# Retention and a mish feed-forward layer in one kernel: chunk steps of the first tiles reordered, states evacuated by ScalarE, four more chunks transposed by TensorE, the last tile's outputs in swapped banks

## The chip, the cores and the metric

The kernel runs on one core of one Trainium2 chip. The metric is device time in microseconds (us) of one execution. A profiled execution has a span, from its first to its last instruction; its own time is a little longer than the span.

## The reference

Two layers follow each other. The first is a retention layer: attention without softmax, with a causal mask and a decay for each head. Its output, as 4608 tokens of 512 features, goes through a feed-forward layer with the activation mish, h * tanh(softplus(h)).

```python
# q, k, v: (8 batches, 8 heads, 576 positions, 64), float32
scores = scale * q @ k.T                                # scale = 1/sqrt(64)
gamma = 1.0 - 2.0 ** (-5.0 - arange(8))
Dmat = where(i >= j, gamma ** (i - j), 0.0)
x = ((scores * Dmat) @ v).transpose(0, 2, 1, 3).reshape(4608, 512)
h = x @ w_in                                            # 512 -> 2048
out = (h * tanh(softplus(h))) @ w_out                   # 2048 -> 512
```

## The kernel before

**Chunks and tiles.** The tokens are cut into 36 chunks of up to 128 positions. A chunk holds all eight heads. Each batch has four chunks of 128 (c = 0 to 3); the remaining 64 positions of two neighbouring batches share a fifth (c = 4). Four chunks make a tile of 512 tokens, so there are nine tiles, 0 to 8; chunk n belongs to tile n // 4.

**The decay.** gamma ** (i - j) is split into a factor for q, gamma ** i (`gq`), and one for v, gamma ** -j (`gv`). What is left for the scores is the plain causal mask, and what earlier chunks give to a later one is a running state k.T v for each head, 64 x 64, summed in one PSUM bank, `st`.

**The steps of a chunk n.** They are small functions, and `att(n, "PSKO")` calls those that its letters name:

- P (`prep`): GpSimd (POOL) casts k into `qks`, VectorE (DVE) scales q into `qks`, GpSimd scales v into `vs`. For n over 8, P also issues the loads of up to two later chunks, as far as chunk n + 7 (`more_loads`).
- T (`step_t`): q and k are transposed, two heads at a time, into `qkT`. For n below `NPE` = 12 TensorE does it in eight matmuls with the identity, into a PSUM bank (from the pool `hp` for tile 0, from `sc` later), and ScalarE (ACT) copies the result (L183). For other chunks a DMA transpose, issued by ScalarE, does it (L185).
- S (`step_s`): eight matmuls give the scores in two PSUM banks (`sc`, one of two such pairs), and VectorE multiplies them by the mask into `sm` (L200).
- K (`step_k`): eight matmuls add this chunk to the state in `st`. VectorE reads `st` and writes `ssb` (L221): of each pair of heads, one copy where the lower half of the partitions is zeroed, one where the upper half is, by a multiplication with `diag`. The next K may not write `st` before that read is done. Chunks with c = 4 have no K.
- O (`step_o`): for c > 0 eight matmuls (sixteen for c = 4) multiply the earlier state by the transposed q, and eight multiply `sm` by `vs`, all into the first `sc` bank. VectorE copies the result into `xT`, the tile's input of the feed-forward layer (L246).

**The feed-forward layer.** `g1(t, f)` multiplies tile t by 128 columns of w_in, four matmuls of 512 columns into a bank `hp` (one of two), and ScalarE takes the mish of it into `gT` (L259). `g2(t, i)` is a quarter of one chunk's product with w_out, four matmuls into the bank `ops`, and after the last quarter VectorE copies the result to `res` (one of three) and SyncE (SP) issues the store (L280). In the last tile, 8, every second chunk's output goes to an `hp` bank instead of `ops`.

**Order.** Everything is in the order in which the code is written: each engine runs its instructions in that order, and each of SP's DMA issues waits for its turn and for its inputs. There are five parts:

1. Attention of tile 0, chunk by chunk.
2. All of `g1(0, ...)`, with the casts of w_in, by GpSimd, between them.
3. The f loop (L328): the products of the first three chunks of tile 0 with w_out, in the order in which w_out's eight pieces arrive and are cast (L115), one piece for two steps; three banks collect the sums. The steps of chunks 4 to 7 stand between them, four values of f for a chunk.
4. Tile 1: the last quarter of tile 0's product (`g2(0, 12)` to `g2(0, 15)`), and `g1(1, ...)` with the steps of chunks 8 to 11.
5. Tiles 2 to 8, and a last round without `g1`: `g1(t, i)` and `g2(t - 1, i)` alternate, and the steps of two chunks of tile t + 1 stand in each half of 16 rounds.

Of the kernel before, what the change touches and what calls it, by code (L numbers as in the profile page):

```python
# [12 lines left out]
AX = mybir.ActivationFunctionType  # L13
OP = mybir.AluOpType
# [3 lines left out]
def kernel(  # L18
# [25 lines left out]
    nF = d_ff // P  # L44
    KC = d_model // P
    NCH = 4
    NPE = 12


    chunks = []  # L50
# [5 lines left out]
    nT = len(chunks) // NCH  # L56
# [8 lines left out]
    op = ctx.enter_context(tc.tile_pool(name="op", bufs=3))  # L65
# [85 lines left out]
    diag = consts.tile([P, 2], F32)  # L151
# [7 lines left out]
    live = {}  # L159
    xts = {}  # L160

    def prep(n):
        b, c = chunks[n]
        qr, kr, vr = raw.pop(n)
        qks = tok.tile([P, 2, H, D], BF16, name="qks")
        vs = tok.tile([P, H, D], BF16, name="vs")
        nc.gpsimd.tensor_copy(qks[:, 1], kr)  # L167
        nc.vector.tensor_tensor(qks[:, 0], qr, gq[:, c, :].unsqueeze(2).to_broadcast([P, H, D]), op=OP.mult)  # L168
        nc.gpsimd.tensor_tensor(vs, vr, gv[:, c, :].unsqueeze(2).to_broadcast([P, H, D]), op=OP.mult)  # L169
        live[n] = (qks, vs)  # L170

    def step_t(n):
        qks, vs = live[n]
        flat = qks.rearrange("p i h d -> p (i h d)")
        qk = tr.tile([P, 2, NP, P], BF16, name="qkT", bufs=5)
        if n < NPE:
            if n < NCH:
                tp = ps_h.tile([P, 2 * NP, P], BF16, name="hp")
            else:
                tp = ps_sc.tile([P, 4 * NP, P], BF16, name="sc")[:, 0:2 * NP]  # L180
            for i in range(2 * NP):
                nc.tensor.transpose(tp[:, i, :], flat[:, ts(i, P)], ident)  # L182
            nc.scalar.copy(qk.rearrange("p i n t -> p (i n) t"), tp)  # L183
        else:
            nc.scalar.dma_start_transpose(out=qk.rearrange("p i n t -> p (i n) t"), in_=flat)  # L185
        live[n] = (qk, qks[:, 1], vs)

    def step_s(n):

        b, c = chunks[n]  # L190
        qk, ks, vs = live[n]
        sc = ps_sc.tile([P, 2, NP, P], F32, name="sc")
        for p in range(NP):
            for e in range(2):
                r = ds(64 * e, 64)
                nc.tensor.matmul(sc[:, e, p, :], lhsT=qk[r, 1, p, :], rhs=qk[r, 0, p, :],  # L196
                                 start=True, stop=True)
# [5 lines left out]
        live[n] = (qk, ks, vs, sc, sm)  # L203

    def step_k(n):

        if n >= len(chunks):
            return
        b, c = chunks[n]
        if c == 4:  # L210
            return
        ks, vs = live[n][1:3]
        if c == 0:
            st_ps[b] = ps_st.tile([P, NP, 64], F32, name="st")
        st = st_ps[b]
        for p in range(NP):
            for e in range(2):
                nc.tensor.matmul(st[ds(64 * e, 64), p, :], lhsT=ks[:, 2 * p + e, :], rhs=vs[:, 2 * p + e, :],  # L218
                                 start=(c == 0 and p == 0), stop=True, skip_group_check=True)
        ssb = tr.tile([P, NP, 2, 64], BF16, name="ssb", bufs=8)  # L220
        nc.vector.tensor_tensor(  # L221
            ssb, st.unsqueeze(2).to_broadcast([P, NP, 2, 64]),
            diag.unsqueeze(1).unsqueeze(3).to_broadcast([P, NP, 2, 64]), op=OP.mult)
        st_sb[b, c] = ssb

    def step_o(n):

        b, c = chunks[n]
        t, s = divmod(n, NCH)
        qk, ks, vs, sc, sm = live.pop(n)  # L230
# [13 lines left out]
        if s == 0:  # L244
            xts[t] = xp.tile([P, KC, NCH * P], BF16, name="xT")
        nc.vector.tensor_copy(xts[t][:, :, ts(s, P)], ot)  # L246
# [14 lines left out]
    def g2(t, i):  # L261
        s, part = divmod(i, 4)
        if part == 0:
            if t == nT - 1 and s % 2:
                outs[t] = ps_h.tile([P, d_model], F32, name="hp")
            else:
                outs[t] = ps_o.tile([P, d_model], F32, name="ops")
        ops = outs[t]
        for f in range(4 * part, 4 * part + 4):
            nc.tensor.matmul(ops, lhsT=gts[t][:, f, ts(s, P)], rhs=w_out_t[:, f, :],  # L270
                             start=(f == 0), stop=(f == nF - 1))
        if part == 3:
            store(t, s, ops, nc.vector.tensor_copy)
# [51 lines left out]

    accs = [ps_h.tile([P, NCH * P], F32, name="hp") for _ in range(2)]
    accs += [ps_o.tile([P, d_model], F32, name="ops")]
    for f in range(nF):  # L328
        n, w = NCH + f // 4, f % 4
        if w == 0:  # L330
            att(n, "PT")
        elif w == 1:
            att(n, "SK")
        elif w == 3:
            att(n, "O")
        if f % 2 == 0:
            j = f // 2
            cast_w("out", j)
            if j + STG < 8:
                load_w("out", j + STG)  # L340
            if j == 1 or j > 3 and j != 5:
                more_loads(10, 1)
        for s in range(3):
            nc.tensor.matmul(accs[s], lhsT=gts[0][:, f, ts(s, P)], rhs=w_out_t[:, f, :],
                             start=(f == 0), stop=(f == nF - 1))
    att(2 * NCH, "PT")
    for s in range(3):
        store(0, s, accs[s], nc.vector.tensor_copy if s % 2 else nc.scalar.copy)

    for i in range(nF):  # L350
        n, w = 2 * NCH + i // 4, i % 4
        if i < 4:
            g2(0, 12 + i)
        if w == 0:
            att(n + 1, "P")
            att(n, "SK")
        elif w == 2:
            att(n, "O")
            att(n + 1, "T")
        if n + 2 == NPE + 1:  # L360
            if w == 1:
                att(n + 2, "P")
            elif w == 3:
                att(n + 2, "T")
        g1(1, i)

    for t in range(2, nT + 1):
        for i in range(nF):
            n, w = NCH * (t + 1) + i // 8 * 2, i % 8
            if t < nT:  # L370
                if w == 0:
                    att(n, "S")
                    att(n + 1, "S")
                    if n == NPE:
                        att(n, "K")
                elif w == 1 and n == NPE:
                    att(n + 1, "K")
                if w in (0, 2):
                    att(n + 2 + w // 2, "P")
                elif w in (1, 3):  # L380
                    att(n + 2 + w // 2, "T")
                elif w == 4:
                    att(n + 2, "K")
                    att(n, "O")
                    att(n + 1, "O")
                    att(n + 3, "K")
                g1(t, i)
            g2(t - 1, i)

# [29 lines left out]
```

## Time and the profile before

| | us |
|---|---|
| median of 3 runs | 347.21 (346.68 to 348.35) |
| profiled execution, own time | 347.57 |
| its span | 345.9 |
| TensorE busy (matmuls) | 307.6, 89% of the span |
| VectorE busy | 131.1, 38% |
| ScalarE busy | 100.7, 29% |
| GpSimd busy | 79.0, 23% |
| mean granted clock of TensorE | 0.988 |

Rows of the profile name an instruction by its line in the code, its engine, the tile that it writes and those that it reads. PE is TensorE (PEld its weight loads, which overlap the matmuls), DVE VectorE, ACT ScalarE, POOL GpSimd; SPq and ACTq are DMA issues by SP and ScalarE. A row of the timeline gives the start, the length, the instruction and how many of its kind were merged (x8), and, in brackets, how long the engine had stood idle before it and what ended the wait. A row by stage gives start and end, length, busy time of PE, PEld, DVE, ACT and POOL with their instruction counts, the granted clock, and the mean busy share and rate of the DMA engines. A row of the chain has start, length and instruction only.

### The profile page before, as it was taken

Reading aid. Unit: us, or ns where it says so; the run is one execution under the profiler, and the core shown is the slowest. Engines: PE = TensorE matmul, PEld = TensorE weight load, DVE = VectorE, ACT = ScalarE, POOL = GpSimd, SP = SyncE. Lnnn points to the kernel's source line nnn. Section 1 sums busy time; section 2 is a strip of 40 time slices with the busy share of each in tenths; the row PEclk is TensorE's granted clock in tenths of the full one; section 3 lists DMA queues with packets and bytes.
Section 4 is the critical chain, followed back from the end, with each engine's and each line's share of the span. In section 5 each row is a group of like instructions: output and inputs, shape, how many; then the busy total and the mean of one; then the engine's idle time right before and its main releaser. Section 6 shows DMA issues by size and latency. Waiting matters only on the chain.

```text
span 345.9 us, 5710 instructions
## 1 busy us (share of the span) xinstructions
PE 307.6 (89%) x2336; PEld 148.4 (43%) x2336; DVE 131.1 (38%) x186; ACT 100.7 (29%) x163; POOL 79.0 (23%) x100
## 2 busy tenths in 40 slices
PE   2458988689979996999999999999999999999994
PEld 1343434344534442444444445444554444444441
DVE  2662035615653421635344342434353633001111
ACT  4122641226512232132222323223222232333200
POOL 4566554514411311213030303030301000000000
PEclk9999999989989999999999999999999999999999
DMA  9999999999897989999794949473140411000122
GB/s 172 226 349 260 303 250 246 174 215 204 142 201 127 209 168 254 247 184 204 174 221 108 229 110 203 98 119 89 36 91 32 99 54 31 32 30 30 48 75 61
DMA packets 149530, 52.80 MB, mean 153 GB/s; under 512 B 138752, under 2 KB 142848, under 8 KB 149504
## 3 DMA queue, kind: packets, MB, share of 16 engines
q1 hardware_dynamic: 124160, 46.15, 60.9%
q10 hardware_dynamic: 25344, 6.29, 11.3%
q8 instruction: 18, 0.29, 0.4%
q14 instruction: 8, 0.07, 0.1%
HBM read 36.70 MB, written 9.44 MB: 133 GB/s over the span
## 4 chain that ended last, share of the span: by engine, by line
PE 65%; DMA 13%; SPq 8%; DVE 6%; issue 3%; POOL 2%; ACT 2%; ACTq 1%; DVEq 0%; POOLq 0%
PE hp L257 29%; PE ops L270 27%; SPq L85 7%; DMA wst<-in_moe_w_out_dram 5%; DVE res L277 2%; DMA wst<-in_moe_w_in_dram 2%; PE sc L196 2%; PE hp L270 2%; DMA qkT<-qks 2%; DVE ssb L221 2%; DMA vraw<-in_v_dram 1%; DMA qraw<-in_q_dram 1%; PE st L218 1%; DVE qks L168 1%; DMA out_dram<-res 1%
## 5 line engine op out<-in xcount | busy, mean ns | idle before, releaser
L257 PE MATMUL hp<-xT,w_in_t 128*128 128x512 bf16 x576 | 149.1, 389 | 1.3 <-DVE xT L246 0.8
L259 ACT ACTIVATE gT<-hp 128x512 bf16<-128x512 f32 x144 | 84.9, 597 | 187.3 <-PE hp L257 166.9
L270 PE MATMUL ops<-w_out_t,gT 128*128 128x512 bf16 x496 | 127.2, 381 | 6.3 <-DVE res L277 4.2
L257 PEld LDWEIGHTS <-w_in_t 128*128 128x128 bf16 x576 | 54.6, 99 | 67.0 <-issue 7.2
L270 PEld LDWEIGHTS <-gT 128*128 128x128 bf16 x528 | 52.0, 98 | 70.4 <-issue 10.0
L277 DVE COPY res<-ops 128x512 f32<-128x512 f32 x31 | 21.5, 692 | 149.4 <-PE ops L270 139.6
L169 POOL TENSOR_TENSOR vs<-vraw,gv 128x512 bf16<-128x512 f32 x36 | 38.0, 1057 | 127.6 <-issue 66.2
L200 DVE TENSOR_TENSOR sm<-sc,mask 128x1024 bf16<-128x1024 f32 x36 | 43.0, 1219 | 34.8 <-PE sc L196 34.7
L167 POOL CAST qks<-kraw 128x512 bf16<-128x512 f32 x36 | 23.2, 644 | 42.3 <-DMA kraw<-in_k_dram 31.2
L246 DVE CAST xT<-sc 128x512 bf16<-128x512 f32 x36 | 23.7, 685 | 13.7 <-PE sc L242 13.7
L168 DVE TENSOR_TENSOR qks<-qraw,gq 128x512 bf16<-128x512 f32 x36 | 24.8, 711 | 4.6 <-DMA qraw<-in_q_dram 4.6
L221 DVE TENSOR_TENSOR ssb<-st,diag 128x512 bf16<-128x512 f32 x32 | 21.8, 682 | 0.9 <-PE st L218 0.9
L196 PE MATMUL sc<-qkT 64*128 64x128 bf16 x288 | 13.6, 232 | 6.2 <-ACT qkT L183 3.5
L196 PEld LDWEIGHTS <-qkT 64*128 64x128 bf16 x288 | 8.8, 100 | 16.2 <-ACT qkT L183 6.7
L182 PE MATMUL hp<-ident,qks 128*128 128x128 bf16 x32 | 4.3, 310 | 12.6 <-DVE qks L168 11.9
L242 PE MATMUL sc<-sm,vs 128*64 128x128 bf16 x288 | 14.6, 230 | 0.0
L182 PEld LDWEIGHTS <-qks 128*128 128x128 bf16 x96 | 6.7, 111 | 18.4 <-DVE qks L168 16.9
L183 ACT COPY qkT<-sc 128x1024 bf16<-128x1024 bf16 x8 | 8.1, 1011 | 21.4 <-PE sc L182 21.4
L218 PE MATMUL st<-vs,qks 128*64 128x64 bf16 x256 | 10.6, 207 | 3.7 <-DVE ssb L221 3.7
L237 PE MATMUL sc<-qkT,ssb 128*64 128x128 bf16 (+1 forms) x256 | 12.0, 224 | 1.0 <-DVE sm L200 1.0
L218 PEld LDWEIGHTS <-qks 128*64 128x64 bf16 x256 | 7.2, 116 | 11.1 <-issue 10.4
L242 PEld LDWEIGHTS <-vs 128*64 128x64 bf16 x288 | 10.6, 117 | 1.0 <-issue 1.0
(34 smaller groups left out, 71.1 us busy)
## 6 DMA issues: line engine op xcount, KB each, us to landing
qraw<-in_q_dram SPq DMA_DIRECT2D x32, 256.0 KB, 5.0
kraw<-in_k_dram SPq DMA_DIRECT2D x32, 256.0 KB, 5.1
vraw<-in_v_dram SPq DMA_DIRECT2D x32, 256.0 KB, 5.1
out_dram<-res SPq DMA_DIRECT2D x32, 256.0 KB, 2.2
wst<-in_moe_w_in_dram SPq DMA_DIRECT2D x8, 512.0 KB, 6.1
wst<-in_moe_w_out_dram SPq DMA_DIRECT2D x8, 512.0 KB, 5.3
qraw<-in_q_dram SPq DMA_DIRECT2D x8, 128.0 KB, 4.2
kraw<-in_k_dram SPq DMA_DIRECT2D x8, 128.0 KB, 4.0
```

Source lines behind the costliest of these rows:

```text
L85: nc.sync.dma_start(out=t, in_=src[b, :, ds(P * c, P), :].rearrange("h p d -> p h d"))
L168: nc.vector.tensor_tensor(qks[:, 0], qr, gq[:, c, :].unsqueeze(2).to_broadcast([P, H, D]), op=OP.mult)
L169: nc.gpsimd.tensor_tensor(vs, vr, gv[:, c, :].unsqueeze(2).to_broadcast([P, H, D]), op=OP.mult)
L196: nc.tensor.matmul(sc[:, e, p, :], lhsT=qk[r, 1, p, :], rhs=qk[r, 0, p, :], start=True, stop=True)
L200: nc.vector.tensor_tensor(sm.rearrange("p e n i -> p (e n) i"), sc.rearrange("p e n i -> p (e n) i"), m.unsqueeze(1).to_broadcast([P, 2 * ...
L221: nc.vector.tensor_tensor(ssb, st.unsqueeze(2).to_broadcast([P, NP, 2, 64]), diag.unsqueeze(1).unsqueeze(3).to_broadcast([P, NP, 2, 64]), ...
L242: nc.tensor.matmul(ot[ds(64 * e, 64), p, :], lhsT=vs[:, 2 * p + e, :], rhs=sm[:, e, p, :], start=(c == 0 and p == 0), stop=True, skip_grou ...
L246: nc.vector.tensor_copy(xts[t][:, :, ts(s, P)], ot)
L257: nc.tensor.matmul(hp, lhsT=w_in_t[:, c, ts(f, P)], rhs=xts[t][:, c, :], start=(c == 0), stop=(c == KC - 1))
L259: nc.scalar.activation(gts[t][:, f, :], hp, AX.Mish)
L270: nc.tensor.matmul(ops, lhsT=gts[t][:, f, ts(s, P)], rhs=w_out_t[:, f, :], start=(f == 0), stop=(f == nF - 1))
L277: copy(ot, ops)
```

## The change

There are four edits:

- **Order of the chunk steps** in tiles 0 to 2. In tile 0 the next chunk's P stands ahead of a chunk's S and K, and its T ahead of the O. In the f loop and in tile 1, a chunk's T, S with K, and the next chunk's P stand at the four steps of a round, and its O follows at the second step of the next round. In tile 2's first half, chunks 12 and 13 get T, S and K there, and chunks 14 and 15 P, K and T.
- **States**: `ssb` is written by two ScalarE ACTIVATEs with the function Copy, one for each column of `diag` as a scale, in place of one VectorE multiplication (L222 after, L221 before).
- **NPE** is 16: chunks 12 to 15 are transposed by TensorE too, through an `sc` bank and a ScalarE copy, in place of DMA transposes.
- **Last tile**: chunks 0 and 2 of tile 8, not 1 and 3, take an `hp` bank.

```diff
-    NPE = 12
+    NPE = 16
...
-        nc.vector.tensor_tensor(
-            ssb, st.unsqueeze(2).to_broadcast([P, NP, 2, 64]),
-            diag.unsqueeze(1).unsqueeze(3).to_broadcast([P, NP, 2, 64]), op=OP.mult)
+        for e in range(2):
+            nc.scalar.activation(ssb[:, :, e, :], st, AX.Copy, scale=diag[:, e:e + 1])
...
-            if t == nT - 1 and s % 2:
+            if t == nT - 1 and s % 2 == 0:
                 outs[t] = ps_h.tile([P, d_model], F32, name="hp")
...
+    att(0, "PT")
     for n in range(NCH):
-        att(n, "PT")
-        if n > 0:
-            att(n - 1, "O")
+        if n + 1 < NCH:
+            att(n + 1, "P")
         att(n, "SK")
-    att(NCH - 1, "O")
+        if n + 1 < NCH:
+            att(n + 1, "T")
+        att(n, "O")
...
+    att(NCH, "P")
     for f in range(nF):
         n, w = NCH + f // 4, f % 4
         if w == 0:
-            att(n, "PT")
+            att(n, "T")
         elif w == 1:
+            if n > NCH:
+                att(n - 1, "O")
+        elif w == 2:
             att(n, "SK")
-        elif w == 3:
-            att(n, "O")
+        elif n < 2 * NCH - 1:
+            att(n + 1, "P")
...
-    att(2 * NCH, "PT")
     for s in range(3):
         store(0, s, accs[s], nc.vector.tensor_copy if s % 2 else nc.scalar.copy)
 
     for i in range(nF):
         n, w = 2 * NCH + i // 4, i % 4
-        if i < 4:
-            g2(0, 12 + i)
+        if i == 0:
+            att(n, "P")
+            g2(0, 12)
+            att(n - 1, "O")
+            g2(0, 13)
+            g2(0, 14)
+        elif i == 1:
+            g2(0, 15)
         if w == 0:
+            att(n, "T")
+        elif w == 1:
+            if i > 4:
+                att(n - 1, "O")
+        elif w == 2:
+            att(n, "SK")
+        else:
             att(n + 1, "P")
-            att(n, "SK")
-        elif w == 2:
-            att(n, "O")
-            att(n + 1, "T")
-        if n + 2 == NPE + 1:
-            if w == 1:
-                att(n + 2, "P")
-            elif w == 3:
-                att(n + 2, "T")
         g1(1, i)
+    att(3 * NCH - 1, "O")
 
     for t in range(2, nT + 1):
         for i in range(nF):
             n, w = NCH * (t + 1) + i // 8 * 2, i % 8
-            if t < nT:
+            if t == nT:
+                pass
+            elif n == 3 * NCH:
+                steps = {0: ((n, "T"), (n + 1, "P")), 1: ((n + 1, "T"), (n, "K")),
+                         3: ((n, "S"), (n + 1, "S"), (n + 1, "K")), 2: ((n + 2, "P"),), 4: ((n + 3, "P"),),
+                         6: ((n + 2, "K"), (n, "O"), (n + 1, "O"), (n + 3, "K"), (n + 2, "T")),
+                         7: ((n + 3, "T"),)}
+                for m, step in steps.get(w, ()):
+                    att(m, step)
+            else:
                 if w == 0:
                     att(n, "S")
                     att(n + 1, "S")
-                    if n == NPE:
-                        att(n, "K")
-                elif w == 1 and n == NPE:
-                    att(n + 1, "K")
...
```

The rest of the diff keeps what the steps pass on in a dictionary for each chunk, so that K can come before S.

**VectorE, tile 0.** The first rows after the setup, before the change:

```order
L168 TENSOR_TENSOR qks<-qraw,gq 128x512
L200 TENSOR_TENSOR sm<-sc,mask 128x1024
L221 TENSOR_TENSOR ssb<-st,diag 128x512
L168 TENSOR_TENSOR qks<-qraw,gq 128x512
L246 CAST xT<-sc 128x4x128
L200 TENSOR_TENSOR sm<-sc,mask 128x1024
L221 TENSOR_TENSOR ssb<-st,diag 128x512
```

And after it:

```order
L168 TENSOR_TENSOR qks<-qraw,gq 128x512 x2
L200 TENSOR_TENSOR sm<-sc,mask 128x1024
L246 CAST xT<-sc 128x4x128
L168 TENSOR_TENSOR qks<-qraw,gq 128x512
L200 TENSOR_TENSOR sm<-sc,mask 128x1024
L246 CAST xT<-sc 128x4x128
```

The scaling of the next chunk's q now stands ahead of a chunk's mask product, and the state is gone from this engine.

**ScalarE, from the f loop to the end of tile 1** (`qkT` copies are T, `ssb` is the state, `gT` mish, `res` the stores of tile 0). Before:

```order
L183 COPY qkT<-sc 128x1024 x5
L277 COPY res<-hp 128x512
L277 COPY res<-ops 128x512
L259 ACTIVATE gT<-hp 128x512 x2
L183 COPY qkT<-sc 128x1024
L259 ACTIVATE gT<-hp 128x512 x4
```

After, beginning at the last T of the f loop:

```order
L183 COPY qkT<-sc 128x1024
L222 ACTIVATE ssb<-st,diag 128x4x64 x2
L277 COPY res<-hp 128x512
L277 COPY res<-ops 128x512
L183 COPY qkT<-sc 128x1024
L259 ACTIVATE gT<-hp 128x512 x4
L183 COPY qkT<-sc 128x1024
L259 ACTIVATE gT<-hp 128x512 x2
L222 ACTIVATE ssb<-st,diag 128x4x64 x2
L259 ACTIVATE gT<-hp 128x512 x2
```

The copy of chunk 8, the fifth of the row x5, has moved behind the two stores, and in tile 1 each four mish now share the engine with one copy and two ACTIVATEs of a state.

**SP, from the stores of tile 0 on.** The difference:

```order
-L280 DMA out_dram<-res 128x512 x3
+L280 DMA out_dram<-res 128x512 x4
 L85 DMA qraw<-in_q_dram 128x8x64
 L85 DMA kraw<-in_k_dram 128x8x64
```

All four stores of tile 0 now stand ahead of the loads of chunk 11; SP's rows ahead of these, and all rows of GpSimd, are those of before.

More of the change, by code (lines that the diff above doesn't have):

```diff
@@ L169, in prep @@
         nc.gpsimd.tensor_tensor(vs, vr, gv[:, c, :].unsqueeze(2).to_broadcast([P, H, D]), op=OP.mult)
-        live[n] = (qks, vs)
+        live[n] = {"qks": qks, "ks": qks[:, 1], "vs": vs}
     def step_t(n):
-        qks, vs = live[n]
+        qks = live[n]["qks"]
         flat = qks.rearrange("p i h d -> p (i h d)")
@@ L185, in step_t @@
             nc.scalar.dma_start_transpose(out=qk.rearrange("p i n t -> p (i n) t"), in_=flat)
-        live[n] = (qk, qks[:, 1], vs)
+        live[n]["qk"] = qk
     def step_s(n):
         b, c = chunks[n]
-        qk, ks, vs = live[n]
+        qk = live[n]["qk"]
         sc = ps_sc.tile([P, 2, NP, P], F32, name="sc")
@@ L202, in step_s @@
             m.unsqueeze(1).to_broadcast([P, 2 * NP, P]), op=OP.mult)
-        live[n] = (qk, ks, vs, sc, sm)
+        live[n].update(sc=sc, sm=sm)
     def step_k(n):
@@ L211, in step_k @@
             return
-        ks, vs = live[n][1:3]
+        ks, vs = live[n]["ks"], live[n]["vs"]
         if c == 0:
@@ L229, in step_o @@
         t, s = divmod(n, NCH)
-        qk, ks, vs, sc, sm = live.pop(n)
+        qk, vs, sc, sm = (live[n][x] for x in ("qk", "vs", "sc", "sm"))
+        del live[n]
         ot = sc[:, 0]
@@ L386 @@
                     att(n + 3, "K")
+            if t < nT:
                 g1(t, i)
```

## The prediction

> **What bounds the kernel now.** I read the page's first two parts, then busy time by stage, the chain, the timeline at each seam, and the waits of the SP queue. By stage (length, then busy time of each engine, clock, DMA share):
>
> ```profile
> 0.00:28.00 28.00, 11.80 (x153) 8.57 (x154) 14.18 (x28) 7.18 (x9) 14.65 (x26) 1.00 1.12 256
> 28.00:44.70 16.70, 16.70 (x68) 7.05 (x68) 0.69 (x1) 8.96 (x15) 10.24 (x11) 1.00 1.12 268
> 44.70:70.27 25.57, 18.90 (x208) 9.21 (x206) 13.77 (x18) 6.53 (x8) 13.13 (x14) 1.00 0.97 214
> 70.27:99.33 29.06, 26.62 (x248) 12.94 (x248) 13.92 (x18) 12.30 (x19) 8.00 (x9) 0.93 1.00 194
> 99.33:132.59 33.26, 32.69 (x236) 15.13 (x233) 13.54 (x19) 9.44 (x16) 9.89 (x12) 0.96 0.98 179
> 132.59:169.72 37.13, 32.36 (x257) 15.46 (x257) 14.47 (x20) 9.34 (x16) 6.32 (x9) 1.00 1.07 221
> 169.72:327.41 157.69, 154.60 (x1114) 73.83 (x1114) 57.77 (x79) 47.00 (x80) 16.80 (x21) 1.00 0.45 93
> ```
>
> Cuts lie at the start of a stage's first matmul (the last two at the scores of chunks 16 and 20). The stages are: attention of tile 0; its first product; its second (the f loop); tiles 1, 2, 3; tiles 4 to 8. After 169.72 TensorE is full and DMA half idle, so nothing but TensorE work counts there. Before it TensorE stands still for about 16 us in the start, 7 in the f loop, 2 in tile 1 and 5 in tile 3, while DMA is busy throughout. So each gain must come before 169.72, and may not come sooner than DMA delivers.
>
> **Start.** Chunk 3, and what it waits for:
>
> ```profile
> 16.28 0.61 POOL L167 CAST qks<-kraw 128x512 bf16<-128x512 f32 x1 [1.35 <-DMA kraw<-in_k_dram]
> 20.22 0.68 DVE L221 TENSOR_TENSOR ssb<-st,diag 128x512 bf16<-128x512 f32 x1
> 20.82 1.20 DVE L168 TENSOR_TENSOR qks<-qraw,gq 128x512 bf16<-128x512 f32 x1
> 22.07 1.04 PE L182 MATMUL hp<-ident,qks 128*128 128x128 bf16 x8 [2.68 <-DVE qks L168]
> 27.99 16.70 PE L257 MATMUL hp<-xT,w_in_t 128*128 128x512 bf16 x64 [0.78 <-DVE xT L246]
> ```
>
> Chunk 3's k is cast at 16.89, yet its transposes start at 22.07, because q's scaling stands on VectorE behind the mask product and the state of chunk 2. The change puts that scaling ahead and takes the state away. Then the transposes start at 16.9, the chain behind them stays (22.07 to 27.99, 5.9), and the first product starts near 22.8. I count these 5.2 us as nothing, since the f loop, next, waits for DMA:
>
> ```profile
> 49.52 2.47 POOL L115 CAST w_out_t<-wst 128x1024 bf16<-128x1024 f32 x2 [1.66 <-DMA wst<-in_moe_w_out_dram]
> 55.88 1.04 POOL L115 CAST w_out_t<-wst 128x1024 bf16<-128x1024 f32 x1 [0.96 <-DMA wst<-in_moe_w_out_dram]
> 58.09 1.04 POOL L115 CAST w_out_t<-wst 128x1024 bf16<-128x1024 f32 x1 [1.16 <-DMA wst<-in_moe_w_out_dram]
> 61.74 0.62 PE L182 MATMUL sc<-ident,qks 128*128 128x128 bf16 x8 [0.75 <-DVE qks L168]
> 66.50 0.38 PE L344 MATMUL ops<-w_out_t,gT 128*128 128x512 bf16 x1
> 69.61 0.61 ACT L277 COPY res<-ops 128x512 f32<-128x512 f32 x1
> 70.27 1.10 PE L270 MATMUL ops<-w_out_t,gT 128*128 128x512 bf16 x4 [2.13 <-ACT res L277]
> ```
>
> **f loop.** SP's and POOL's order up to the last piece of w_out is unchanged and each cast waits for DMA, so the last piece is still cast at 59.13. Before, the loop runs on to 66.7 (66.50 and 0.22 to the next), because a chunk's whole chain (scaling, transposes, copy, scores, mask, output, xT) stands in one round of four steps: chunk 7's transposes come only at 61.74, behind their scaling. Afterwards O(n-1) moves into the next round and the scaling P(n+1) a step ahead, so no round holds the chain. Six products remain after 59.13: 1.3 at full pace, half that pace 2.6. With the last scores and states ahead of them I take 60.9; ends 60.4 and 63.9 (all that follows the cast of 55.88 at half pace). The two paces, four matmuls each:
>
> ```profile
> 71.91 1.82 PE hp L257 x4
> 104.51 0.86 PE hp L257 x4
> ```
>
> **Seam to tile 1.** Before, ScalarE's two stores queue behind the copy of chunk 8, so TensorE waits 2.13 us. Now that copy stands behind the stores: about 1.0 us after 60.9, g2 resumes at 61.9. Three parts of g2 (3 x 0.86), O(7), T(8), hand-offs 0.4: g1(1,0) at 65.8 where it was 71.9, with two more g2 parts already done. A T costs 0.45, the distance of the first two starts; O(7) I take alike:
>
> ```profile
> 83.19 0.62 PE L182 MATMUL sc<-ident,qks 128*128 128x128 bf16 x8
> 83.64 1.89 PE L257 MATMUL hp<-xT,w_in_t 128*128 128x512 bf16 x8
> 98.44 0.61 PE L196 MATMUL sc<-qkT 64*128 64x128 bf16 x8 [1.44 <-DMA qkT<-qks]
> 99.33 1.89 PE L257 MATMUL hp<-xT,w_in_t 128*128 128x512 bf16 x4
> ```
>
> **Tile 1.** An ordinary half of a later tile takes 16.37 (186.09 to 202.46, quoted under tile 3); its sixteen parts of products take 13.82, so a chunk's scores, states and outputs cost 1.27 with their stalls. Here: sixteen g1 and one g2 part, 14.7; four T, 1.8; four chunks, 5.1; and 0.7 for xT(11), which now stands right ahead of the next tile (a VectorE copy of the length of ssb, 0.68): 22.3, so g1(2,0) at 88.1 for 99.33. The wait for two DMA transposes (1.44 shown above, then g1 at half pace) is gone. ScalarE's load per chunk is four Mish, one copy, one pair of states:
>
> ```profile
> L259 ACT ACTIVATE gT<-hp 128x512 bf16<-128x512 f32 x144 | 84.9, 597 | 187.3 <-PE hp L257 166.9 <-DVE qks L168 13.8 <-PE st L218 3.8
> L183 ACT COPY qkT<-sc 128x1024 bf16<-128x1024 bf16 x8 | 8.1, 1011 | 21.4 <-PE sc L182 21.4
> L137 ACT ACTIVATE gq<-ex 128x40 f32<-128x40 f32 x1 | 0.2, 236 | 0.4 <-DVE ex L134 0.4
> L221 DVE TENSOR_TENSOR ssb<-st,diag 128x512 bf16<-128x512 f32 x32 | 21.8, 682 | 0.9 <-PE st L218 0.9
> ```
>
> A state ACTIVATE has 256 elements; no row shows one. It lies between 236 (40 elements) and 597 ns (512); I take the line between them, 401, so a pair 0.80 us, ends 0.47 and 1.19. That makes 2.39 + 1.01 + 0.80 = 4.2 us of ScalarE in the 5.2 of a chunk: tight. Upper end 25: a Mish behind a copy frees hp late by 1.01 less the 0.26 between a part (0.86) and a Mish (0.60), 0.75 a chunk, if nothing hides it. Lower end 20.5: the chunk's stalls, some 0.4, hidden. Stores of tile 0 stand on SP ahead of chunk 11's loads; the fourth now waits for its copy near 68, still earlier than before, when the third store waited for a copy until 70.2 and the loads came behind.
>
> The Trainium skill, page "ScalarE: Activation LUTs", section "Rules for kernel authors", speaks against this edit: multiplications belong on VectorE. By its section "What ACT_TABLE_LOAD costs" (186 ns, 0.833 per element, 93 per pointer operand, 93 overlap) a pair is an estimated 0.89 us, which would make the sum about 0.4 us worse in tile 1; by the row it is 0.80. No run here shows it yet.
>
> **Tile 2.** Two ordinary halves, 32.7; T(13) to T(15), 1.35; 0.7 for two states more and for T(14), which takes xT(12)'s bank and waits for it: 34.7, longer than the 33.3 of before. S(16) at 122.8 for 132.59. So the four transposes moved to TensorE cost 1.8 us (T(12) counted in tile 1) where TensorE is the bound.
>
> **Tile 3.**
>
> ```profile
> 132.62 1.50 SPq L280 DMA_DIRECT2D out_dram<-res  x2
> 136.84 0.69 DVE L277 COPY res<-ops 128x512 f32<-128x512 f32 x1 [9.81 <-DMA out_dram<-res]
> 137.58 1.02 PE L270 MATMUL ops<-w_out_t,gT 128*128 128x512 bf16 x4 [3.40 <-DVE res L277]
> 153.05 0.62 PE L196 MATMUL sc<-qkT 64*128 64x128 bf16 x16
> 186.09 0.62 PE L196 MATMUL sc<-qkT 64*128 64x128 bf16 x16
> 202.46 0.62 PE L196 MATMUL sc<-qkT 64*128 64x128 bf16 x16
> SPq L85 <- DMA qkT<-qks: 21.4, 4, 7.8
> ```
>
> This half took 20.46 (132.59 to 153.05), an ordinary one 16.37. Its three result buffers were full: two stores went out only at 132.62, since SP stood behind loads that waited 21.4 us for DMA transposes. Without four of these, and with the first store one load earlier, it should leave near 117 and be needed near 123. I take two ordinary halves: S(20) at 155.6 for 169.72, 14.1 us.
>
> **Rest.**
>
> ```profile
> 162.46 0.32 PE L218 MATMUL st<-vs,qks 128*64 128x64 bf16 x8 [0.56 <-DVE ssb L221]
> PE st L218 <- DVE ssb L221: 3.7, 8, 0.6
> 327.41 3.61 PE L270 MATMUL ops<-w_out_t,gT 128*128 128x512 bf16 x16 [0.78 <-DVE res L277]
> 167.24 0.60 ACT L259 ACTIVATE gT<-hp 128x512 bf16<-128x512 f32 x1 [1.13 <-PE hp L257]
> ```
>
> The second state of a half waits up to 0.56 for VectorE, where a result copy stands ahead. On ScalarE a Mish stands ahead and the pair is 0.12 longer: gain 0.5 of 3.7 in all (ends: 3.7 gained, 2.5 lost). ScalarE's idle 1.13 between two Mish takes the pair, so that costs nothing; were it longer, Mish would free hp late and g1 would wait. The last tile's first output needs no result copy: 0.78 gained. The second, in ops, has 3.6 us of matmuls between that copy and itself.
>
> **Sum.** 14.1 + 0.5 + 0.8 = 15.4. The profiled execution took 347.57 us (span 345.9): 332.2. The median of the runs shown, 347.21, lies 0.36 lower: 331.8, rounded to 332. A difference under 0.5% (1.7 us) can't be told from none.
>
> **Rivals.**
> - ScalarE crowds tile 1: Mish and copy hold up hp, 25 instead of 22.3. Its load of 4.2 in 5.2 speaks for it, the two hp buffers against. 334.5; chance 0.14.
> - The store jam of tile 3 stays, since T(16) and T(17) still go by DMA and SP still waits for them: 4.1 us back, 336; 0.12. Against it: the store needed next now leaves before chunk 22's loads.
> - The clock falls while the f loop waits for weights (some 4 us until 49.52's cast): it ends at 63.9, 335; 0.10. For it: after the 2.13 us wait at 70.27 g1 ran at 1.82 instead of 0.86. The Trainium skill ("TensorE: Matmul & The Clock Gate", Part 1) has a window of about 3.4 us without work; the trace shows the fall after less.
> - The f loop keeps its end, because chunk steps and not weights hold it: the change would not do there what its order says. 5.8 back, 337.5; 0.07. Against it: O(n-1) and S(n) no longer share a round.
> - States on ScalarE come later than on VectorE, and each K waits: 0.3 more in 12 halves, 336; 0.06.
> - Slower than before: the pair and Mish no longer fit, and TensorE waits for hp at all 32 states. To eat 15.4 + 1.7 us each must cost 0.54, so a pair of 1.13 + 0.54, about 1.7 us: then 349 or more. The 597 ns of twice the elements speak against; 0.03.
>
> **How the numbers follow.** The forecast, 329.5 to 334, has 0.42; better than that, by short stalls in tile 1 or the 3.7 us of states, 0.06. 328 to 338.5 holds all single rivals but the last and leaves out some 0.15 for two together and the ends. All but the last are faster by far more than 1.7 us: faster 0.95, same 0.02, slower 0.03.
>
> **What would show it.** First g1 near 23; the f loop ending near 61, its last cast unmoved at 58 to 59; g1(2,0) near 88; no DMA transposes before S(14); no wait of VectorE for out_dram; states on ScalarE near 0.4 us each; the tiles from 4 on 157 us long. A last cast that moves, a Mish that TensorE waits for in every chunk of tile 1, or tile 3 over 33 us would make me wrong.

## The result, and the profile after

The changed kernel takes 333.55 us (median of 4 runs, 332.08 to 335.12), the one before 347.78 beside it: a ratio of 0.9585, 95% interval 0.9515 to 0.9656. The forecast was 332.0. The profiled execution after took 334.6 us, with a span of 332.9. By stage of that execution, cut as before (length; busy time of PE, PEld, DVE, ACT, POOL; granted clock, DMA share and rate; the last row stops 18.5 us short of the end of the span, as that of before did):

```profile
0.00:22.28 22.28, 12.19 (x152) 8.30 (x153) 11.18 (x24) 10.54 (x17) 10.06 (x22) 1.00 1.13 233
22.28:39.28 17.00, 16.73 (x71) 7.40 (x73) 0.77 (x1) 9.21 (x16) 10.03 (x11) 1.00 0.98 267
39.28:64.76 25.48, 19.28 (x177) 9.07 (x178) 10.55 (x12) 8.72 (x15) 12.84 (x15) 0.87 1.00 245
64.76:91.43 26.67, 25.16 (x252) 12.77 (x256) 12.00 (x16) 15.76 (x27) 10.31 (x13) 1.00 0.95 214
91.43:126.14 34.71, 33.46 (x275) 16.84 (x280) 12.99 (x16) 17.02 (x30) 11.93 (x14) 1.00 1.14 208
126.14:158.50 32.36, 31.48 (x255) 15.44 (x258) 12.18 (x16) 12.70 (x24) 6.31 (x8) 1.00 1.10 200
158.50:314.40 155.90, 153.12 (x1096) 73.90 (x1115) 50.36 (x67) 57.08 (x104) 16.80 (x21) 1.00 0.48 97
```

Against the stages of before: the first product starts 5.7 us sooner, the f loop with its seam is as long as it was (25.48 for 25.57), so g2 resumes 5.5 sooner. Tile 1 gives 2.4 (26.67 for 29.06), tile 2 costs 1.45 (34.71 for 33.26), tile 3 gives 4.8 (32.36 for 37.13), and from the scores of chunk 20 to the end of the span it is 174.4 for 176.2. The f loop's clock is 0.87, and the timeline shows why. Rows are start, length, instruction and, in brackets, the idle time ahead and its releaser:

```profile
53.14 1.01 PE L350 MATMUL hp<-w_out_t,gT 128*128 128x512 bf16 x2 [3.19 <-POOL w_out_t L115]
59.86 1.04 POOL L115 CAST w_out_t<-wst 128x1024 bf16<-128x1024 f32 x1 [1.07 <-DMA wst<-in_moe_w_out_dram]
63.65 0.38 PE L350 MATMUL ops<-w_out_t,gT 128*128 128x512 bf16 x1
64.76 1.02 PE L270 MATMUL ops<-w_out_t,gT 128*128 128x512 bf16 x4 [0.73 <-ACT res L277]
```

TensorE stood for 3.19 us until a late piece of w_out was cast, then two matmuls of 512 columns took 1.01 instead of 0.59. The loop's last matmul starts at 63.65 (its end, 0.22 to the next, is 63.87), and g2 resumes 0.89 later, where before that hand-off took 3.55 (66.72 to 70.27).

The chunk steps of tile 1 show a wait that the forecast didn't have:

```profile
67.37 5.28 SPq L280 DMA_DIRECT2D out_dram<-res  x4
71.59 0.69 DVE L277 COPY res<-ops 128x512 f32<-128x512 f32 x1 [4.51 <-PE sc L196]
72.20 1.21 DVE L200 TENSOR_TENSOR sm<-sc,mask 128x1024 bf16<-128x1024 f32 x1
73.33 0.68 DVE L168 TENSOR_TENSOR qks<-qraw,gq 128x512 bf16<-128x512 f32 x1
74.07 0.62 PE L182 MATMUL sc<-ident,qks 128*128 128x128 bf16 x8 [0.69 <-DVE qks L168]
```

Tile 0's fourth result copy starts only at 71.59. There are three `res` buffers, and the first of the three stores that hold them was issued at 67.37, behind chunk 10's loads. The row names the scores as releaser, which the copy doesn't read; at the same place in another run (e2, below) the row names `out_dram`. Behind the copy on VectorE stand chunk 8's mask product and chunk 9's scaling, and TensorE waits for the latter.

The states:

```profile
L222 ACT ACTIVATE ssb<-st,diag 128x256 bf16<-128x256 f32 x64 | 26.9, 471 | 25.2 <-PE st L218 25.0
PE st L218 <- ACT ssb L222: 1.7, 5, 0.4
77.74 0.84 ACT L222 ACTIVATE ssb<-st,diag 128x256 bf16<-128x256 f32 x2
```

An ACTIVATE of 256 elements takes 471 ns, a pair 0.84, and TensorE waits 1.7 us for states where it waited 3.7.

### The profile page after: what moved, and what is told of

It reads as the page before. It is cut to its first block, busy times and chain, and to the rows that moved or that the text cites. A ratio compares the mean times of both kernels' runs of the same rounds, so it can differ in the third digit from the quotient of the medians.

```text
span 332.9 us, 5759 instructions
## 1 busy us (share of the span) xinstructions
PE 305.1 (92%) x2329; PEld 149.8 (45%) x2368; DVE 113.5 (34%) x154; ACT 131.0 (39%) x231; POOL 78.3 (24%) x100
## 4 chain that ended last, share of the span: by engine, by line
PE 74%; SPq 9%; DMA 7%; issue 3%; DVE 3%; ACT 1%; POOL 1%; ACTq 1%; DVEq 0%; POOLq 0%
PE hp L257 31%; PE ops L270 30%; SPq L85 7%; DMA wst<-in_moe_w_out_dram 3%; DMA wst<-in_moe_w_in_dram 3%; PE sc L196 2%; PE hp L270 2%; PE st L218 2%; PE sc L237 2%; PE sc L242 1%; PE hp L350 1%; ACT ssb L222 1%; DVE sm L200 1%; PE sc L182 1%; DMA out_dram<-res 1%
## 5 line engine op out<-in xcount | busy, mean ns | idle before, releaser
L257 PE MATMUL hp<-xT,w_in_t 128*128 128x512 bf16 x544 | 143.4, 385 | 3.9 <-issue 1.3
L270 PE MATMUL ops<-w_out_t,gT 128*128 128x512 bf16 x493 | 125.8, 379 | 1.2 <-ACT res L277 0.7
L222 ACT ACTIVATE ssb<-st,diag 128x256 bf16<-128x256 f32 x64 | 26.9, 471 | 25.2 <-PE st L218 25.0
L168 DVE TENSOR_TENSOR qks<-qraw,gq 128x512 bf16<-128x512 f32 x36 | 25.7, 739 | 14.0 <-DMA qraw<-in_q_dram 14.0
L167 POOL CAST qks<-kraw 128x512 bf16<-128x512 f32 x36 | 22.5, 624 | 30.3 <-DMA kraw<-in_k_dram 26.7
L183 ACT COPY qkT<-sc 128x1024 bf16<-128x1024 bf16 x12 | 12.1, 1012 | 12.4 <-PE sc L182 12.2
L196 PE MATMUL sc<-qkT 64*128 64x128 bf16 x288 | 13.3, 230 | 1.9 <-ACT qkT L183 1.6
L182 PEld LDWEIGHTS <-qks 128*128 128x128 bf16 x128 | 8.5, 106 | 13.7 <-DVE qks L168 9.8
L350 PE MATMUL hp<-w_out_t,gT 128*128 128x512 bf16 x29 | 10.1, 419 | 4.1 <-POOL w_out_t L115 3.5
```

What stands on the lines that cost most here:

```text
L222: nc.scalar.activation(ssb[:, :, e, :], st, AX.Copy, scale=diag[:, e:e + 1])
L257: nc.tensor.matmul(hp, lhsT=w_in_t[:, c, ts(f, P)], rhs=xts[t][:, c, :], start=(c == 0), stop=(c == KC - 1))
```

## The experiments

The marks below are read from each kernel's own profiled execution, in us: the end of w_out's last cast, the end of the f loop (its last start plus 0.22), g2's resumption, the first product of tile 2, the scores of chunks 16 and 20, and the span.

| kernel | last cast | loop ends | g2 | tile 2 | S(16) | S(20) | span |
|---|---|---|---|---|---|---|---|
| before | 59.13 | 66.7 | 70.27 | 99.33 | 132.59 | 169.72 | 345.9 |
| changed | 60.90 | 63.9 | 64.76 | 91.43 | 126.14 | 158.50 | 332.9 |
| e1, changed again | 59.30 | 61.1 | 61.99 | 89.65 | 123.82 | 156.25 | 330.7 |
| e12, changed, third time | 60.37 | 62.1 | 63.02 | 90.84 | 125.08 | 157.42 | 331.8 |
| e2, start undone | 59.13 | 61.4 | 62.32 | 89.62 | 123.79 | 156.14 | 330.6 |
| e3, f loop undone | 60.46 | 62.5 | 63.37 | 90.33 | 124.49 | 156.84 | 331.2 |
| e9, both undone | 58.07 | 65.5 | 66.37 | 91.55 | 125.85 | 158.24 | 332.6 |
| e4, chunk 7 not loaded | 55.68 | 61.1 | 62.03 | 87.88 | 122.15 | 154.49 | 328.8 |
| e10, six buffers | 59.42 | 61.5 | 62.39 | 88.24 | 122.34 | 155.59 | 330.1 |
| e5, states on VectorE | 60.20 | 63.3 | 64.23 | 91.83 | 126.66 | 159.52 | 335.0 |
| e6, DMA transposes | 60.81 | 62.9 | 63.79 | 90.94 | 126.62 | 158.95 | 333.2 |

**The same kernel again (e1, e12).** No edit.

> The changed kernel once more, nothing edited. In its first profile the last piece of w_out was cast at 59.86 us, 1.8 later than in the profile of before (58.09), and the f loop ended at 63.9 where 60.9 was forecast. Theory: the arrival of w_out moves by 1 to 2 us from run to run whatever the kernel, and the loop's end moves with it; a second profile then has another last cast, and the loop's end 3.5 to 4.5 us behind its start. Rival: the new order itself delays the loads; the last cast is then at 59.5 to 60.2 again. Time 332 to 335 by both.

> The changed kernel once more, beside the three others, as their measure: 332 to 334.5; the last cast of w_out lies between 58.2 and 59.9, and the f loop ends at 61 to 64, later where one of TensorE's waits for a cast is over 2 us. Against this: a time that doesn't follow the last cast.

Measured: 333.46 us (332.37 to 333.91; ratio 0.9563, 0.9525 to 0.9601) and 332.55 (331.37 to 334.31; 0.9550, 0.9508 to 0.9592). The last cast and the loop's end in e1:

```profile
58.26 1.04 POOL L115 CAST w_out_t<-wst 128x1024 bf16<-128x1024 f32 x1 [1.16 <-DMA wst<-in_moe_w_out_dram]
60.88 0.38 PE L350 MATMUL ops<-w_out_t,gT 128*128 128x512 bf16 x1
```

The weights arrive at other times in other executions of one program: the last cast began at 59.86, 58.26 and 59.33, and the loop ended 3.0, 1.8 and 1.8 us after its end. The three spans follow in the same order. So the 63.9 of the first profile is arrival and clock, not the order. Two points of the expectations fell: e1's loop ended 2.8 us after its last cast began, not 3.5 to 4.5, and e12 had a wait of 2.56 us for a cast, but kept its pace (below).

**The start, the f loop, and both (e2, e3, e9).** Each puts back the order of before at that place and keeps the rest of the change. In e3 and e9, O(7) goes back with it, from tile 1 to the loop.

```diff
     # e2: tile 0
-    att(0, "PT")
     for n in range(NCH):
-        ...
+        att(n, "PT")
+        if n > 0: att(n - 1, "O")
+        att(n, "SK")
+    att(NCH - 1, "O")
     # e3: f loop
-    att(NCH, "P")
         if w == 0:
-            att(n, "T")
-        ...
+            att(n, "PT")
+        elif w == 1: att(n, "SK")
+        elif w == 3: att(n, "O")
     # e9: e2 and e3
```

> Only the order of the chunk steps in tile 0 is that of before. Theory: the first product starts about 5 us later (near 27.5 instead of 22.3), but the f loop waits for w_out anyway, so the loop still ends with the last cast plus about 4 us, and the time is that of the changed kernel within 1 us. Rival: the earlier start is part of the gain, and the time is 4 to 5 us longer (337 to 339).

> Only the order of the chunk steps in the f loop is that of before (all four steps of a chunk in its own round; O(7) at the loop's end); tile 1 and the rest are those of the changed kernel. Theory: the chain of a chunk again stands in one round, the loop ends at 66 to 67 instead of 63.9, and the time grows by 2 to 4 us (335 to 338). Rival: w_out alone sets the loop's end, and nothing changes (within 1 us).

> Both orders of before at once: tile 0's chunk steps and the f loop's; tile 1 and all the rest as changed. Theory (either order alone brings the f loop's end forward, because the weights arrive at the same time and the chunk rounds only hold the loop when it starts late and each round holds a whole chain): the f loop starts near 42 and ends at 64 to 66.5, not at 61 to 62.5 as with one of the two undone; scores of chunk 20 near 159 to 161, time 335.5 to 338. Rival (neither order matters, the earlier end came from the states on ScalarE and from the arrival of the weights): end at 61 to 62.5, time 332.5 to 333.5.

Measured: 332.51 us (331.76 to 333.06; ratio 0.9539), 333.03 (332.45 to 333.53; 0.9555) and 333.05 (332.63 to 336.91; 0.9581, 0.9532 to 0.9629). None differs from the changed kernel: the theories of a longer time in e3 and e9 fell. e9's rows, from the loop's first matmul to tile 2:

```profile
43.85 0.78 PE L344 MATMUL hp<-w_out_t,gT 128*128 128x512 bf16 x2
57.03 1.04 POOL L115 CAST w_out_t<-wst 128x1024 bf16<-128x1024 f32 x1 [0.49 <-DMA wst<-in_moe_w_out_dram]
65.26 0.38 PE L344 MATMUL ops<-w_out_t,gT 128*128 128x512 bf16 x1
71.39 0.69 DVE L277 COPY res<-ops 128x512 f32<-128x512 f32 x1 [4.12 <-PE ops L270]
91.55 1.04 PE L257 MATMUL hp<-xT,w_in_t 128*128 128x512 bf16 x4 [0.24 <-DVE xT L246]
```

The theory of e9 was right on the loop and wrong on the time. With a late start and whole chains in each round the loop runs 21.6 us from its start, as before (44.97 to 66.7 is 21.7), and ends 7.4 us after the last cast; either new order alone lets it end with the weights. But then tile 1 takes it back. e9's loop ends 3.4 us after e12's, tile 2 starts 0.7 later. In e12 the fourth result copy waits:

```profile
66.57 5.28 SPq L280 DMA_DIRECT2D out_dram<-res  x4
70.80 0.69 DVE L277 COPY res<-ops 128x512 f32<-128x512 f32 x1 [5.45 <-PE hp L257]
90.84 1.04 PE L257 MATMUL hp<-xT,w_in_t 128*128 128x512 bf16 x4 [0.24 <-DVE xT L246]
```

In e9 the copy at 71.39 follows its own g2, without a wait. So the store's place on SP, not the f loop, sets when tile 1 may go on. What the new orders of start and loop are worth together can't be told from nothing: e9's tile 2 starts 0.1, 1.9 and 0.7 us later than in the three profiles of the changed kernel, and its median lies 0.5 above e12's. This holds in e2 as well, whose row names the store:

```profile
69.66 0.69 DVE L277 COPY res<-ops 128x512 f32<-128x512 f32 x1 [5.01 <-DMA out_dram<-res]
```

**Less to load (e4).** Chunk 7 uses chunk 6's data, and its load is left out.

```diff
     def load(n):
+        if n == 7:
+            raw[n] = raw[n - 1]
+            return
```

> The changed kernel without the loads of chunk 7: it works on chunk 6's q, k and v instead, so 786 KB less stand ahead of the last two pieces of w_out. Theory (w_out's arrival sets the loop's end): the last two casts and the loop's end come 3 to 3.6 us earlier, and the time falls by about 3 us (329 to 331). Rival (the chunk steps hold the loop): casts earlier, but the loop's end and the time as in the changed kernel within 1 us.

Measured: 330.01 us (329.07 to 330.46; ratio 0.9465), 3.45 below e1 of the same runs (1.9 in the profiled spans). The size was as the theory said, the place was not: the last cast ends 3.6 us sooner than e1's, yet the loop ends at 61.1 in both. A wait of 2.20 us dropped the clock (second fence: stretches of 2 us, columns as in the stages; the clock stands third from the end):

```profile
50.88 0.59 PE L353 MATMUL hp<-w_out_t,gT 128*128 128x512 bf16 x2 [2.20 <-POOL w_out_t L118]
62.77 6.00 SPq L283 DMA_DIRECT2D out_dram<-res  x4
```

```profile
50.00:52.00 2.00, 1.12 (x7) 0.38 (x8) 0.00 (x0) 0.00 (x0) 1.71 (x2) 0.84 1.03 392
52.00:54.00 2.00, 2.00 (x19) 0.92 (x15) 0.69 (x1) 0.00 (x0) 2.00 (x4) 0.50 1.21 276
54.00:56.00 2.00, 2.00 (x22) 1.05 (x22) 1.15 (x2) 0.84 (x2) 1.68 (x2) 0.81 1.36 187
```

The gain came in tile 1: with the queue a chunk shorter, the stores left at 62.77 and the fourth copy was not held, so tile 2 began 1.8 us sooner. That is nearly all of the 1.9 in the spans; where the rest of the 3.45 between the medians comes from, these two profiles don't show.

**More result buffers (e10).**

```diff
-    op = ctx.enter_context(tc.tile_pool(name="op", bufs=3))
+    op = ctx.enter_context(tc.tile_pool(name="op", bufs=6))
```

> The changed kernel with six result buffers (res) in place of three. Theory (in tile 1 the fourth result copy of tile 0 waits 4.5 to 5.5 us for a store that stands on SP behind chunk 10's loads, and VectorE's mask product of chunk 8 and q scaling of chunk 9 queue behind it): that wait of VectorE for out_dram is gone, the scores of chunk 9 come 5.3 and not 5.9 to 6.9 us after those of chunk 8, and the time is 0.6 to 1.5 us below the changed kernel of the same runs. Rival (the scores of chunk 9 wait for its loads, and a gain there is taken back by those of chunks 10 to 12): same time within 0.5 us.

Measured: 332.27 us (331.22 to 333.33; ratio 0.9539, 0.9496 to 0.9582) beside e12's 332.55. The wait went as the theory said, and what it gave was partly taken back as the rival said, two tiles later instead of in tile 1:

```profile
68.03 0.69 DVE L277 COPY res<-ops 128x512 f32<-128x512 f32 x1 [3.31 <-PE ops L270]
88.24 1.04 PE L257 MATMUL hp<-xT,w_in_t 128*128 128x512 bf16 x4 [0.24 <-DVE xT L246]
142.32 2.16 ACTq L185 DMA_TRANSPOSE qkT<-qks  x1
145.18 1.02 PE L257 MATMUL hp<-xT,w_in_t 128*128 128x512 bf16 x4 [0.77 <-ACT gT L259]
```

The fourth copy runs at 68.03, right behind its g2, and from g2's resumption to tile 2 it takes 25.85 for e12's 27.82. In tile 3 a DMA transpose's issue holds ScalarE for 2.16 us, a mish is late, TensorE waits 0.77, and that tile takes 33.25 instead of 32.34. The profiled span is 1.7 shorter than e12's, the median 0.3, less than the scatter of the runs and than the 0.6 that the theory said. It is no better version that can be measured.

**Tile 1's order undone (e11).**

```diff
+    att(2 * NCH - 1, "O")
+    att(2 * NCH, "PT")
     for s in range(3):
         store(0, s, accs[s], ...)
...
-        if i == 0: ...            # g2(0, 12..15) in two steps
+        if i < 4: g2(0, 12 + i)
         if w == 0:
-            att(n, "T")
-        ...
+            att(n + 1, "P")
+            att(n, "SK")
+        elif w == 2:
+            att(n, "O")
+            att(n + 1, "T")
...
-    att(3 * NCH - 1, "O")
...                           # tile 2, step 0: no T(12), which tile 1 now has
```

> The order of before in tile 1 alone: chunk 7's output and chunk 8's scaling and transposes ahead of tile 0's stores, one quarter of the last g2 in each of four steps, scores with states and the next scaling in one step, output with the next transposes in another, chunk 12 transposed there; all the rest as changed, TensorE's transposes up to chunk 15 included. Theory (tile 3's jam of stores went with tile 1's and 2's order, since all four stores of tile 0 then leave ahead of chunk 11's loads): SP waits as before, the jam of some 4 us in tile 3 returns in part, the wait of TensorE for the stores' copies at the seam (2.1 us, and half pace behind it) returns, time 336 to 340. Rival (the jam went with the four DMA transposes or with the earlier f loop, and tile 1's order is worth only the seam): tile 3 at 32.4 to 33, time 334 to 335.5.

Measured: 336.52 us (334.66 to 337.63; ratio 0.9653, 0.9608 to 0.9697), 4.0 above e12 of the same runs.

```profile
65.41 0.62 PE L182 MATMUL sc<-ident,qks 128*128 128x128 bf16 x8 [1.39 <-DVE qks L168]
68.16 0.59 PE L270 MATMUL ops<-w_out_t,gT 128*128 128x512 bf16 x1 [2.13 <-ACT res L277]
127.85 0.62 PE L196 MATMUL sc<-qkT 64*128 64x128 bf16 x16
160.76 0.62 PE L196 MATMUL sc<-qkT 64*128 64x128 bf16 x16
```

The seam's wait of 2.13 us is back to the hundredth: chunk 8's copy stands ahead of the stores on ScalarE. Tile 3 takes 32.91, without the jam. So the theory's time and its seam were right, but not the return of the jam (VectorE's wait for a result buffer in tile 3, and TensorE's behind it); the rival had the jam right and the time too low. In the profiles e11 is 3.4 behind e12: 1.2 of it at the loop's end, where weights and clock differ from run to run, 1.6 from there to S(16), and 0.6 in tile 3.

**DMA transposes for chunks 12 to 15 (e6).**

```diff
-    NPE = 16
+    NPE = 12
```

> Only NPE is 12 again: chunks 12 to 15 go by DMA transposes, at the changed kernel's places. Theory: TensorE saves 1.8 us of matmuls in tiles 1 and 2, but SP's loads wait for the four transposes, the stores of tile 1 leave late, VectorE waits for a result buffer in tile 3 as before, and the time is 1 to 4 us longer (334 to 338). Rival: at the new places the transposes hold nothing up, and the kernel is 1 to 2 us faster than the changed one (331 to 332).

Measured: 334.7 us (333.41 to 335.08; ratio 0.9565, 0.9520 to 0.9609), the changed kernel's ratio. SP's first store of tile 1 and the scores of chunk 16, then the store in e11 with the result copy that needs its buffer, then the store of the changed kernel:

```profile
122.26 1.28 SPq L280 DMA_DIRECT2D out_dram<-res  x1
126.62 0.62 PE L196 MATMUL sc<-qkT 64*128 64x128 bf16 x16
```

```profile
123.48 1.06 SPq L280 DMA_DIRECT2D out_dram<-res  x1
127.95 0.69 DVE L277 COPY res<-ops 128x512 f32<-128x512 f32 x1 [6.17 <-PE ops L270]
```

```profile
118.05 0.87 SPq L280 DMA_DIRECT2D out_dram<-res  x1
```

The store leaves 4.4 us ahead of S(16) here and in e11, 8.1 in the changed kernel; before, two left at 132.62, the start of S(16). Tile 3 takes 32.3, 32.9 and 32.4, and took 37.1. So undone by itself, neither the transposes on TensorE nor tile 1's order brings the jam back. But each takes 3.7 us of what the store has to spare, and little is left: where the copy waited for the store it ran 4.2 us (before) and 4.5 us (e8, below) after it, and here (at 126.72) and in e11 it runs 4.5 after it. The two were not undone together, so a part of either in the end of the jam is not excluded. What e6, e11 and the changed kernel share is that this store stands on SP ahead of chunk 22's loads, which it stood behind; that comes from tile 2's steps. That place was not undone by itself, and e8 has it and the jam too, so it is not enough. Both expectations fell: no wait came back in tile 3, and in tile 2 the DMA transposes save nothing but cost 1.0 to 1.5 (35.7 for 34.2 to 34.7), which the kernel's time doesn't show.

**States on VectorE (e5), last bank undone (e7).**

```diff
     # e5
-        for e in range(2):
-            nc.scalar.activation(ssb[:, :, e, :], st, AX.Copy, scale=diag[:, e:e + 1])
+        nc.vector.tensor_tensor(ssb, st..., diag..., op=OP.mult)
     # e7
-            if t == nT - 1 and s % 2 == 0:
+            if t == nT - 1 and s % 2:
```

> Only the states are written by VectorE again, by one multiplication. Theory: each half of the tiles from 4 on takes 16.37 us again instead of 16.17, since the state stands behind a result copy on VectorE; over 8 to 10 halves 1.3 to 2 us longer in all, and tile 1 at most 0.5 us shorter because ScalarE has more room; time 334 to 335.5. Rival: ScalarE's pair of states crowds tile 1 in the changed kernel, so tile 1 gets 2 us shorter and the time is below the changed kernel's.

> Only the last tile's banks are those of before. Theory: the first output of the last tile waits 0.78 us for VectorE's copy of the output ahead of it, and nothing else moves. Rival: no wait, or another of the same size elsewhere.

Measured: e5 336.77 us (336.1 to 337.15; ratio 0.9628, 0.9578 to 0.9678), 1.5 to 2.7 us above the changed kernel by the ratios (0.9550 to 0.9585), whose intervals overlap with e5's. The theory had 1.3 to 2; its 334 to 335.5 was passed, with the kernel before at 349.38 in these runs. In e5's profile tile 3 takes 32.86 for 32.34 to 32.43, and from S(20) to the span's end it takes 175.5 for 174.4. Tile 1 is no shorter, and in the changed kernel's tile 1 TensorE waits for no mish, so ScalarE did not crowd it. e7 took 335.54 in its one run, and S(16) and S(20) stand within 0.01 of those of the first profile, so the two can be laid side by side: the span is 0.9 longer, and the old wait is back:

```profile
315.13 3.61 PE L270 MATMUL ops<-w_out_t,gT 128*128 128x512 bf16 x16 [0.78 <-DVE res L277]
```

**Tile 1's product ahead of w_out (e8).** Chunks 4 to 7 are loaded ahead of w_out; `g1(1, ...)` runs while w_out is cast, and all of `g2(0, ...)` after it, with the steps of chunks 8 to 11 (its outputs alternate between `hp` and `ops`, not shown).

```diff
-    more_loads(4, 1)
+    more_loads(2 * NCH - 1, NCH)
...
-    for f in range(nF):      # the f loop and tile 1
-        ...
+    att(NCH, "PT")
+    for n in range(NCH, 2 * NCH): ...   # steps as in tile 0
+    for i in range(nF):
+        ...                             # casts of w_out
+        g1(1, i)
+    for i in range(nF):
+        ...                             # steps of chunks 8 to 11
+        g2(0, i)
```

> A new order that the changed kernel's profile suggests: chunks 4 to 7 are loaded ahead of w_out, their steps run right after the first product of tile 0, then the first product of tile 1, which needs no w_out, while w_out arrives; the second product of tile 0 follows with the steps of chunks 8 to 11 between its parts (its outputs alternate between two banks). Theory (TensorE waits in the f loop for w_out): TensorE has 13.8 us of work that needs no w_out, the first product of tile 2 starts at 82 to 86 us instead of 91.4, and the time is 325 to 329. Rival: DMA stays the bound further on, since chunks 8 to 15 arrive no earlier; tile 1 and 2 wait for them, and the gain is under 2 us.

Measured: 341.46 us (340.37 to 342.38; ratio 0.9763), 8 above the changed kernel, 6 to 7 by the ratios; the theory fell, and the rival expected no loss. The first product of tile 1 starts at 53.84, since TensorE now waits for the steps of chunks 4 to 7 instead, in part at half pace (clock 0.67 from 38.25 to 53.84), and tile 2 starts near 91 all the same. In tile 3 (clock 0.91) the jam is back:

```profile
125.76 1.09 SPq L280 DMA_DIRECT2D out_dram<-res  x1
130.24 0.69 DVE L277 COPY res<-ops 128x512 f32<-128x512 f32 x1 [11.13 <-DMA out_dram<-res]
130.99 1.86 PE L270 MATMUL ops<-w_out_t,gT 128*128 128x512 bf16 x4 [4.44 <-DVE res L277]
```

Its first store left at 125.76, 0.6 after S(16), though it stands on SP ahead of chunk 22's loads as in the changed kernel. So the jam goes with the time at which the store leaves: it comes where that is no sooner than S(16), in two kernels, and stays away with 4.4 us to spare or more, in the others with three buffers.

## Why the prediction was right, and where its steps were not

- **Start, worth nothing by itself.** Right: first product at 22.28 (22.8 said), and e2 loses nothing.
- **f loop, 60.9.** The distance from the end of the last cast was right (1.8 in e1 and e12). Mis-sized was the cast, taken as unmoved at 59.13: it ends between 59.30 and 60.90 from run to run (a last cast that moves was among the signs of being wrong). With it the rival of a falling clock came true in one profile: 63.9 and 334.6 us, where it said 63.9 and 335. The failed step is the worth of the term: 5.8 us at the loop's end were carried on in full, but e9, which ends there only 1.2 sooner than before, is as fast.
- **Seam.** Right: 0.89 for 1.0, and e11 brings back the 2.13.
- **Tile 1.** From g2's resumption 26.2 were said; 26.67, 27.66 and 27.82 came in the three profiles. The failed step is "the fourth now waits for its copy near 68": the copy itself waited for a store until 69.8 to 71.6. Without that wait it is 25.85 (e10) and 25.2 (e9). "No wait of VectorE for `out_dram`" was wrong here.
- **Tile 2, 34.7.** 34.71 (34.17 and 34.24 in e1 and e12). The four transposes' 1.8 are a loss only against no transposes; against DMA transposes with their waits they gain 1.0 to 1.5 in this tile.
- **Tile 3, 32.8 without the jam.** 32.36. The reason given, without four DMA transposes and with the first store a load earlier, is in part open: the store left near 117 as said (116.3 to 118.1), but without the first half of the reason it still leaves in time (e6), and both halves together are not enough (e8).
- **States.** A pair takes 0.84 where 0.80 was said. The Trainium skill, "ScalarE: Activation LUTs", "What ACT_TABLE_LOAD costs", gave 0.89; the trace lies between the two. Its section "Rules for kernel authors", multiplications on VectorE, is not borne out for this edit: e5 is slower by about 2 us. The gain from S(20) on was put at 0.5; against e5 it is 1.1, and 0.5 more in tile 3.
- **Last bank, 0.78.** e7's span says 0.9, in its one run.

The sum, of the first profile against its forecast of 332.2: loop's end +3.0, seam -0.1, tile 1 +0.5, tile 2 0, tile 3 -0.4, the rest -0.5, together +2.4, which is 334.6. By e12's profile the same terms are +1.2, -0.1, +1.6, -0.5, -0.5 and -0.5: what came out longer in the loop and in tile 1 was half made up by what came out shorter behind them, so that the time came as close as it did is in part luck. Against before, e9's span is shorter by tile 3 (4.7), tile 1 (3.9), the seam (2.7), the rest (1.8) and the loop (1.2), and tile 2 costs 1.0: 13.3 in all. Some of tile 1's 3.9 only moved over the line between the stages: before, S(12) and S(13), with waits of 1.00 and 1.44 for DMA transposes, stood ahead of tile 2's first product, and now they stand behind it. Why tile 1 is shorter was not taken apart beyond that and e11.

## What to carry to other kernels

A gain at one stage's end is only worth what the next stage can take: look for the wait that will hold there whatever came before, here a store behind loads on one in-order queue with three buffers. Undo two edits that serve the same end together as well as one by one, since each alone may seem worthless. And take the profile of the same program twice before a late transfer is explained by an edit.

## What the runs showed of the hardware

The clock did not fall by the length of a wait alone. TensorE ran at half pace after waits of 1.69 (e6), 2.13 (before, and e11), 2.20 (e4) and 3.19 us (the changed kernel), and at full pace after 2.56 in e12 and 3.40 in the kernel before (its row at 137.58, under the prediction's tile 3: four matmuls in 1.02). The rows of e6 and e12, two matmuls each:

```profile
51.52 0.98 PE L350 MATMUL hp<-w_out_t,gT 128*128 128x512 bf16 x2 [1.69 <-POOL w_out_t L115]
```

```profile
51.91 0.59 PE L350 MATMUL hp<-w_out_t,gT 128*128 128x512 bf16 x2 [2.56 <-POOL w_out_t L115]
```

Once it fell, it stayed so for 3.4 us in e4 and for twice that in the changed kernel: e4's three stretches above lack 0.16, 0.50 and 0.19 of the clock for 2 us each, which makes 1.7 / 0.5 = 3.4 us at half pace, and the changed kernel's clock is 0.66 from 50 to 60 us, which makes 3.4 / 0.5 = 6.8. The Trainium skill, "TensorE: Matmul & The Clock Gate", Part 1, has a window of 3.4 us that runs freely, so that it matters where in the window a wait falls: that agrees with the 3.4 and 6.8 us and with 2.56 and 3.40 having done nothing where 1.69 did. That it takes a whole window without work does not agree, since 1.69 us was enough.
